# Keys and values of a linear attention in seven block products, sums formed in filled PSUM banks, and reciprocals in a compact form

## The chip, the cores and the metric

The kernel runs on one core of a Trainium2 chip. The metric is the device time of one execution in microseconds (us); three runs of the kernel before took 2869.28 to 2871.71 us, with a median of 2870.33.

## The reference

Two attention blocks over the same sequence (2048 tokens, width 1024, 32 heads of 32) are mixed by a gate for each token. All of it is in 32-bit floats.

```python
def _A_ref(x, wqkv, wo):                       # linear attention
    q, k, v = qkv[0], qkv[1], qkv[2]           # from x @ wqkv
    phi = lambda t: jnp.where(t > 0, t + 1, jnp.exp(t)) + 1e-6
    pq, pk = phi(q), phi(k)
    kv = jnp.einsum("bhsd,bhse->bhde", pk, v)
    z = jnp.einsum("bhsd->bhd", pk)
    num = jnp.einsum("bhqd,bhde->bhqe", pq, kv)
    den = jnp.einsum("bhqd,bhd->bhq", pq, z)[..., None] + 1e-6
    return (num / den, heads joined) @ wo
def _B_ref(x, wqkv, wo):                       # softmax attention
    scores = jnp.einsum("bhqd,bhkd->bhqk", q, k) * (Dh ** -0.5)
    p = _softmax(scores, axis=-1)
    return (jnp.einsum("bhqk,bhkd->bhqd", p, v), heads joined) @ wo
x = A_x
g = _sigmoid((x * gate_w).sum(-1, keepdims=True))
return g * _A_ref(x, A_wqkv, A_wo) + (1 - g) * _B_ref(x, B_wqkv, B_wo)
```

## The kernel before

Matmuls against weights are done in three passes: an operand is split into a high part (ScalarE rounds it, L252 or L547) and a low part (VectorE or GpSimd subtracts, L253 or L549), and high by high, high by low and low by high are summed in one bank (L146 to L148 in `three`). One product of a 128-token tile with 512 columns over a depth of 1024 is 8 x 3 = 24 matmuls of 128 x 128 by 128 x 512.

The stages in order:

- *First stage*, to about 400 us: X is loaded transposed and split. The first half of the softmax block's values is made (L446 to L448), and its queries and keys for pairs of 512-token blocks in seven products in place of eight (L407 to L409): the blocks of X are `x11` to `x22`, and four sums of them, `t1` to `t4`, are formed on VectorE and split as well (`v_next`, `v_sums`). The parts of X go to DRAM (`spill`), the sums don't.
- *Linear work*, a stream of chunks (`linear`): the second half of the values (`v`, alone on TensorE to about 525 us), four chunks `kv` of the linear attention (256 columns of keys beside 256 of values, L772 and after), two chunks `q`, two chunks `o` (the linear attention's output, its small matrices having been multiplied into the output weights by `mix`, L649).
- *Heads* (`heads_`, `maxima`), from 525 us on, beside the linear work: for each of 32 heads, 64 matmuls for the scores (L887) of which VectorE takes row maxima (L892); the maxima are turned, and go into two more rows of the queries; 64 matmuls for the transposed scores less the maxima (L1038), of which ScalarE takes exponentials (L1042) into one of seven SBUF tiles `pr` (one for each 128 keys); P·V in groups of five or six of these tiles (L1136, into the fixed bank 4). The row sums: GpSimd adds the first 1536 of 2048 columns of each tile to an accumulator (L1085, L1089), VectorE the rest in bank 7 (L1096, L1098). `finish` multiplies them by ones (L940), so that each of four rows of sums stands on 32 partitions, takes reciprocals of all 128 x 512 in four pieces (L947), multiplies the head's output by them (L950) and stores it (L952).
- *Output* (`output`), from about 2650 us: the softmax block's output projection, the gate and the store.

The order of every engine's instructions is written out ahead by a planner in the kernel. It keeps a clock for each engine (`T`, advanced by `use` with a cost written at each place) and at each step advances that stream (linear, maxima, heads, output) which is furthest behind its aim; `rates` holds how many matmuls of linear work go to one 512-column exponential. VectorE's work that nobody waits for at once is put off (`defer`) and run in a place that `fill` finds, or when its result is wanted (`need`). Six banks (`RING`) are handed out by `take` and given back by `give`. All DMAs are issued by SP, in the order of the program. `load_xp` loads the two split parts of a tile of X two tiles ahead; `load_w` and `split_w` load and split weights; `keys` multiplies phi(k) by v (L584) and adds the result to `kvb` (L593); `load_mix` loads output weights for `mix`, which is not started until 8 us of the planner's time later.

## Time and profile before

| | |
|---|---|
| median of three runs | 2870.33 us |
| the profiled execution | 2873.77 us |
| its span, first to last instruction | 2872.0 us |
| mean granted TensorE clock | 0.996 |
| moved by DMA | 400.57 MB |

In the page, PE is TensorE's matmuls and PEld its weight loads; DVE is VectorE, ACT ScalarE, POOL GpSimd, SP the engine that issues the DMAs. A group of instructions is a line of the kernel, an engine, an operation, and the tiles written and read (`mx<-bank`), with their shapes; behind the count stand the busy time in all, the mean time of one in ns, and how long the engine was idle just before them, with what ended that. An fp32 matmul such as those of L1136 has two records. Matmuls overlap in the records, so that the time of one is longer than the step from one to the next. The chain of waits is followed back from the last instruction, each time to what released it.

### The profile page before, as it was taken

Reading aid. Unit: us, or ns where it says so; the run is one execution under the profiler, and the core shown is the slowest. Engines: PE = TensorE matmul, PEld = TensorE weight load, DVE = VectorE, ACT = ScalarE, POOL = GpSimd, SP = SyncE. Lnnn points to the kernel's source line nnn. Section 1 sums busy time; section 2 is a strip of 40 time slices with the busy share of each in tenths; the row PEclk is TensorE's granted clock in tenths of the full one; section 3 lists DMA queues with packets and bytes.
Section 4 is the critical chain, followed back from the end, with each engine's and each line's share of the span. In section 5 each row is a group of like instructions: output and inputs, shape, how many; then the busy total and the mean of one; then the engine's idle time right before and its main releaser. Section 6 shows DMA issues by size and latency. Waiting matters only on the chain.

```text
span 2872.0 us, 44436 instructions
## 1 busy us (share of the span) xinstructions
PE 2846.1 (99%) x15744; PEld 2036.8 (71%) x15744; DVE 2239.1 (78%) x3775; ACT 1617.8 (56%) x3007; POOL 1854.1 (65%) x646
## 2 busy tenths in 40 slices
PE   9999999999999999999999999899999999999999
PEld 8888888666666666666666666566766666666687
DVE  7667656788888888888888888778888888886643
ACT  5334321666666667666666666566666656656421
POOL 1212220778898889888988887578778877885000
PEclk9999999999999999999999999999999999999999
DMA  5956764332333233333332235554465344524663
GB/s 179 284 174 212 247 201 152 121 93 92 108 89 92 89 101 110 90 92 92 120 93 90 76 120 168 173 185 145 135 195 167 114 137 133 144 88 143 213 219 105
DMA packets 302498, 400.57 MB, mean 139 GB/s; under 512 B 92682, under 2 KB 185354, under 8 KB 299146
## 3 DMA queue, kind: packets, MB, share of 16 engines
q1 hardware_dynamic: 302276, 397.73, 44.8%
q8 instruction: 124, 2.03, 0.3%
q14 instruction: 98, 0.80, 0.1%
HBM read 287.57 MB, written 108.79 MB: 138 GB/s over the span
## 4 chain that ended last, share of the span: by engine, by line
PE 96%; DMA 2%; DVE 1%; ACT 0%; issue 0%; SPq 0%; ACTq 0%; DVEq 0%
PE bank L1038 16%; PE bank L887 16%; PE bank L1136 15%; PE bank L146 11%; PE bank L148 11%; PE bank L147 11%; PE bank L407 4%; PE bank L409 4%; PE bank L408 4%; PE bank L446 1%; PE bank L940 1%; PE bank L447 1%; PE bank L448 1%; DMA big<-xs 1%; PE bank L693 0%; PE bank L584 0%
## 5 line engine op out<-in xcount | busy, mean ns | idle before, releaser
L1089 POOL TENSOR_TENSOR big<-big,big 128x1536 f32<-128x1536 f32 (+1 forms) x434 | 1556.4, 3586 | 188.9 <-ACT big L1042 166.7
L892 DVE TENSOR_REDUCE mx<-bank 128x1 f32<-128x512 f32 x2048 | 1311.4, 681 | 319.6 <-PE bank L887 315.1
L1042 ACT ACTIVATE big<-bank 128x512 f32<-128x512 f32 x2048 | 1180.6, 601 | 524.8 <-PE bank L1038 455.6
L1038 PE MATMUL bank<-big,big 128*128 128x512 f32 x2048 | 810.7, 397 | 2.7 <-ACT big L1042 2.6
L887 PE MATMUL bank<-big,big 128*128 128x512 f32 x2048 | 803.6, 392 | 3.2 <-ACT mid L342 2.9
L146 PE MATMUL bank<-big,big 128*128 128x512 f32 x1408 | 552.7, 393 | 5.7 <-DMA big<-xs 3.4
L148 PE MATMUL bank<-big,big 128*128 128x512 f32 x1408 | 550.9, 391 | 1.0 <-DMA big<-oA 0.6
L147 PE MATMUL bank<-big,big 128*128 128x512 f32 x1408 | 550.6, 391 | 0.0
L1038 PEld LDWEIGHTS bank<-big,big 128*128 128x128 f32 x2048 | 384.6, 188 | 159.7 <-issue 62.0
L1136 PE MATMUL bank<-big,mid 128*32 128x512 f32 x4096 | 461.1, 595 | 0.0
L887 PEld LDWEIGHTS bank<-big,big 128*128 128x128 f32 x2048 | 385.4, 188 | 87.4 <-ACT big L1042 3.7
L1136 PEld LDWEIGHTS bank<-big,mid 128*32 128x32 f32 x4096 | 127.9, 110 | 266.2 <-issue 266.2
L146 PEld LDWEIGHTS bank<-big,big 128*128 128x128 f32 x1408 | 264.6, 188 | 71.0 <-ACT big L1042 4.3
L148 PEld LDWEIGHTS bank<-big,big 128*128 128x128 f32 x1408 | 264.8, 188 | 57.6 <-DMA big<-oA 1.0
L147 PEld LDWEIGHTS bank<-big,big 128*128 128x128 f32 x1408 | 264.5, 188 | 55.3
L1098 DVE TENSOR_TENSOR bank<-bank,big 128x512 f32<-128x512 f32 (+1 forms) x434 | 280.6, 647 | 7.8 <-ACT big L1042 6.1
L1085 POOL TENSOR_TENSOR big<-big,big 128x1536 f32<-128x1536 f32 (+1 forms) x31 | 111.6, 3601 | 253.0 <-ACT big L1042 135.5
L253 DVE TENSOR_TENSOR big<-mid,big 128x512 fp32r<-128x512 f32 x216 | 153.0, 732 | 80.5 <-ACT big L252 80.5
L386 POOL TENSOR_TENSOR mid<-mid,mid 128x512 f32<-128x512 f32 x16 | 20.6, 1291 | 276.7 <-DVE big L253 250.6
L252 ACT CAST big<-mid 128x512 fp32r<-128x512 f32 x216 | 130.2, 624 | 95.8 <-POOL mid L387 54.0
L407 PE MATMUL bank<-big,big 128*128 128x512 f32 x448 | 174.3, 389 | 0.0
L408 PE MATMUL bank<-big,big 128*128 128x512 f32 x448 | 174.3, 389 | 0.0
(103 smaller groups left out, 1981.9 us busy)
## 6 DMA issues: line engine op xcount, KB each, us to landing
big<-xs SPq DMA_DIRECT2D x208, 512.0 KB
qk<-mid SPq DMA_DIRECT2D x128, 256.0 KB
big<-oA SPq DMA_DIRECT2D x64, 512.0 KB
big<-qk SPq DMA_DIRECT2D x96, 256.0 KB
big<-qk SPq DMA_DIRECT2D x384, 64.0 KB
mid<-in_b_wqkv SPq DMA_DIRECT2D x88, 256.0 KB
xs<-big SPq DMA_DIRECT2D x64, 256.0 KB
oA<-mid SPq DMA_DIRECT2D x64, 256.0 KB
```

The lines of the kernel that those rows point to most:

```text
L146: yield nc.tensor.matmul(ps, sh, mh_, start=(kt == 0), stop=False)
L147: yield nc.tensor.matmul(ps, sh, ml_, start=False, stop=False)
L148: yield nc.tensor.matmul(ps, sl, mh_, start=False, stop=(kt == NK - 1))
L407: nc.tensor.matmul(ps, sh, mh_, start=(i == 0), stop=False)
L408: nc.tensor.matmul(ps, sh, ml_, start=False, stop=False)
L887: nc.tensor.matmul(bank[b], q[:, t * P:(t + 1) * P], k[:, j * C:(j + 1) * C], start=True, stop=True)
L892: nc.vector.tensor_reduce(m[:, t, j:j + 1], bank[b], AX.X, ALU.max)
L1038: nc.tensor.matmul(bank[b], k[:, t * P:(t + 1) * P], q[:, j * C:(j + 1) * C], start=True, stop=True)
L1042: nc.scalar.activation(pr_t[i][:, j * C:(j + 1) * C], bank[b], AF.Exp, scale=SCALE)
L1089: nc.gpsimd.tensor_add(lacc[:, :qp], lacc[:, :qp], pr(t)[:, :qp])
L1098: nc.vector.tensor_add(lacc[:, qp:] if t == NT - 1 else l_b[:, :n], l_b[:, :n], src)
L1136: nc.tensor.matmul(av_b[j * DH:(j + 1) * DH, :], v[:, t, :], pr(t)[:, j * C:(j + 1) * C], start=(t == 0), stop=(t == NT - 1))
```

## The change

- *Keys and values.* Two chunks `kv` in place of four, each two old chunks wide (set `s`). Tokens are taken in eight pairs of tiles (`tokens`), 512 tokens apart, so that the parts and sums of X from the first stage serve again; the sums are now also stored (`spill_t`, 64 more stores in the first stage). A set has seven weight operands, `b11`, `b21`, `b22` and the sums `t1` to `t4`, which `w_sums` forms on GpSimd and stores (the first set's during the chunk `v`, the second's during the first set). A product is half as deep: 4 x 3 = 12 matmuls. `ORDER` takes them phase by phase, eight pairs in each.
- *Sums in banks.* The products must be added to each other. Where a sum starts from an earlier one, ScalarE copies that from SBUF into a free bank and the product's matmuls accumulate onto it (`get`, `start` false). A sum that is wanted again is copied out by ScalarE (`copy_u`) and stored to DRAM for a later phase (`load_u` brings it back); two products in every pair and set are added by VectorE (`add_u`). Only a bank that a whole 512-column matmul has written last may be filled so (`whole`). What was done at once behind each `kv` tile (phi, sums of keys) is a stream of its own, `kvout`.
- *Weights* of these products have their low parts taken by VectorE in place of GpSimd.
- *Reciprocals.* For all heads but the last, ScalarE copies the row sums to SBUF, four DMAs take one partition of each row to a tile of 128 x 16, VectorE takes reciprocals of that, a DMA stores them and one brings them back spread over 32 partitions for each row, and GpSimd multiplies the head's output by them (`back`, `scale`).
- *Planner.* Linear work may run ahead by 40 in place of 9; 1.5 matmuls of keys and values go to an exponential; the mixing is started 25 us after its loads in place of 8; VectorE's put-off work goes ahead of a maximum only if it ends 1 us before that can start, in place of 1 us after; between streams that all wait, the lag of ScalarE or VectorE counts too.

The core of the diff:

```diff
-AHEAD = {"head": 0, "max": 6, "lin": 9, "out": 0}
+RATE_KV = 1.5
+AHEAD = {"head": 0, "max": 6, "lin": 40, "kvout": 0, "out": 0}
...
-LATE = 1.0
+LATE = -1.0
...
+    NSET, NPAIR = 2, NT // 2
...
+    def take(seed=False, part=False, kept=False):
+
+        idle = [b for b in RING if not held[b] and (whole[b] or not seed)]
...
         return b
...
+    def spill_t(np_, i):
+
+        def one(name, p):
+            nc.sync.dma_start(xt_d[name][p][np_][:, :, i, :].rearrange("t p c -> p t c"),
+                              f32(xop(name, p, i)).rearrange("p (t c) -> p t c", c=P))
+
+        return [lambda a=(name, p): one(*a) for name in ("t1", "t2", "t3", "t4") for p in range(2)]
...
+    PHASES = ((("b11", "x"), ("b21", "x")), (("t2", "t2"),), (("t3", "t1"), ("t4", "x")), (("t1", "t3"), ("b22", "t4")))
+    WOPS = [op for ph in PHASES for op, _ in ph]
+    JOBS = [(ph, pair) for ph in range(len(PHASES)) for pair in range(NPAIR)]
...
+    def load_op(n, i):
...
+        s, m = divmod(n, len(WOPS))
+        if s == NSET:
+            return load_w("q", 0, m * HK + i, LEAD_W + 1)
+        op = WOPS[m]
+        if op[0] == "b":
+            raw = load_cols(a_wqkv, kv_cols(2 * s + int(op[2]) - 1), (int(op[1]) - 1) * HK + i, LEAD_W + 1)
+        else:
+            raw = raw_tile(LEAD_W + 1)
+            nc.sync.dma_start(raw, wt_d[s][op][i])
+        return raw, T["pe"] + 4.0
...
+    def w_sums(s, i, tiles):
+
+
+        r11, r12, r21, r22 = tiles
+
...
+        def loads():
+            for half, c, r in ((0, 0, r11), (0, 1, r12), (1, 1, r22), (1, 0, r21)):
+                load(r, half, c)
+
+        def add(fn, out, a, b):
+            use("pool", 1.29)
+            fn(out, a, b)
+
+        def store(name, r):
+            nc.sync.dma_start(wt_d[s][name][i], r)
+
+        sub, plus = nc.gpsimd.tensor_sub, nc.gpsimd.tensor_add
+        return ([loads],
+                [lambda: add(sub, r11, r11, r12), lambda: add(plus, r12, r22, r12),
+                 lambda: add(sub, r22, r22, r11), lambda: add(sub, r21, r21, r22)],
+                [lambda n=n, r=r: store(n, r) for n, r in (("t1", r11), ("t3", r12), ("t2", r22), ("t4", r21))])
+
+    w_steps = deque()
...
+    def kv_out(c, b, items=(), at=0.0):
+
+        n = n_kv[0]
+        n_kv[0] += 1
...
+        yield lambda: ended(items)
+        need(items)
+        yield from keys_alone(n - 2)
+        nc.scalar.copy(va, ps[:, HC:])
+        use("act", 0.28, T["pe"] + LATENCY["pe"], ended(items), at)
+        end = phi(ps, e, HC)
...
+    def load_u(what, pair, i):
+        nc.sync.dma_start(u_free(i), u_d[what][pair])
+        u_what[i] = what, pair
+        u_at[i] = T["pe"] + 4.5
+
+    def copy_u(i, b, what, pair):
+        u = u_free(i)
+        u_at[i] = use("act", 0.5, T["pe"] + LATENCY["pe"])
+        nc.scalar.copy(u, bank[b])
+        u_what[i] = what, pair
+        if what in (S1, U2, P7):
+            nc.sync.dma_start(u_d[what][pair], u)
+        return u_at[i]
+
+    def add_u(i, b):
+        item = defer(lambda _: nc.vector.tensor_add(bank[b], bank[b], u_tiles[i]),
+                     max(T["pe"] + LATENCY["pe"], u_at[i]), 0.66, 0)
+        u_left[i].append(item)
+        return item
...
+    ORDER = []
+    for m in range(NPAIR + 1):
+        ORDER += [(0, pr, q) for pr, q in ((0, m), (1, m - 1)) if 0 <= q < NPAIR]
+    ORDER += [(1, 0, q) for q in range(NPAIR)]
+    ORDER += [(2, pr, q) for q in range(NPAIR) for pr in range(2)]
+    for m in range(NPAIR + 1):
+        ORDER += [(3, pr, q) for pr, q in ((0, m), (1, m - 1)) if 0 <= q < NPAIR]
...
+        SEED = {(0, 1): (S1, lambda q: q % 4), (1, 0): (S1, lambda q: q % 4), (2, 1): (U2, lambda q: q % 2 * 2),
+                (3, 0): (U2, lambda q: q % 2 * 2), (3, 1): (W5, lambda q: q % 2 * 2)}
...
+        def get(pi):
+            s, ph, m, pair = XS[pi]
+            seeded = (ph, m) in SEED
+            b = take(seed=seeded)
+            end = free[b]
+            if seeded:
+                what, tile_of = SEED[ph, m]
+                i = tile_of(pair)
+                assert u_what[i] == (what, pair)
+                end = use("act", 0.6, free[b], u_at[i])
+                nc.scalar.copy(bank[b], u_tiles[i])
+            got[pi] = b, seeded, end
...
+            if pi not in got:
+                yield lambda: ready(pi)
+                get(pi)
+            b, seeded, at = got.pop(pi)
...
+                (sh, sl), (wh, wl) = [half_x(pi, p)[:, k] for p in range(2)], [wpart(slot, p) for p in range(2)]
+                for j, (x_, w) in enumerate(((sh, wh), (sh, wl), (sl, wh))):
+                    nc.tensor.matmul(bank[b], x_, w, start=(k == 0 and j == 0 and not seeded),
+                                     stop=(k == HK - 1 and j == 2), skip_group_check=seeded)
+                    lin_pe(1.0)
...
+            load_x(pi + 4)
+            c = 2 * s + (ph == 3)
+            if (ph, m) == (0, 0):
+                give(b, copy_u(pair % 4, b, S1, pair))
+            elif ph == 1:
+                give(b, copy_u(pair % 4, b, U2, pair))
+            elif (ph, m) == (2, 0):
+                give(b, copy_u(pair % 2 * 2 + 1, b, P7, pair))
+            elif (ph, m) == (2, 1):
+                kv_outs.append(kv_out(c, b, [add_u(pair % 2 * 2 + 1, b)]))
+            elif (ph, m) == (3, 0):
+                copy_u(pair % 2 * 2, b, W5, pair)
+                kv_outs.append(kv_out(c, b, [add_u(pair % 2 * 2 + 1, b)], u_at[pair % 2 * 2]))
+            else:
+                kv_outs.append(kv_out(c, b))
...
-        def store(_):
-            nc.vector.tensor_mul(avs, avs, pl)
-            for j in range(NJ):
-                nc.sync.dma_start(oB_d[j * TPC:(j + 1) * TPC, rows, g, :].rearrange("t p c -> p t c"),
-                                  avs[j * DH:(j + 1) * DH, :].rearrange("p (t c) -> p t c", c=P))
...
+        if h < H - 1:
+            part = l_part[h % 2]
+            end = use("act", 0.5, end)
+            nc.scalar.copy(l_sb, pl)
+            give(b, end)
+            for j in range(NJ):
+                nc.sync.dma_start(part[j * DH:(j + 1) * DH, :],
+                                  l_sb[j * DH:j * DH + 1, :].rearrange("o (c e) -> o c e", e=C // DH))
+
+            def back(end):
+                nc.vector.reciprocal(part, part)
+                nc.sync.dma_start(r_d[h % 2].rearrange("j (c e) -> (j c) e", e=C // DH), part)
+                nc.sync.dma_start(l_sb, r_d[h % 2].unsqueeze(1).to_broadcast([NJ, DH, C]))
+                scale_at[0] = end + 6.0
+
+            def scale():
+                need(f_left)
+                use("pool", 1.29)
+                nc.gpsimd.tensor_mul(avs, avs, l_sb)
+                for j in range(NJ):
+                    nc.sync.dma_start(oB_d[j * TPC:(j + 1) * TPC, rows, g, :].rearrange("t p c -> p t c"),
+                                      avs[j * DH:(j + 1) * DH, :].rearrange("p (t c) -> p t c", c=P))
+
+            f_left[:] = [defer(back, end + 4.0, 0.2, 2)]
+            task = (lambda: both(ended(f_left), scale_at[0]), scale)
+            f_task.append(task)
+            tasks.append(task)
+            return
...
-    rates["kv"] = rates["o"] = (cost["kv"] + cost["o"] - RESERVE) / (steps - cost["q"] / RATE_Q)
+    rates["kv"] = RATE_KV
+    rates["o"] = (cost["o"] - RESERVE) / (steps - cost["q"] / RATE_Q - cost["kv"] / RATE_KV)
```

TensorE, keys and values beside heads, before: `bank_249` collects one tile's product (L146 to L148) between scores (L887) and transposed scores (L1038), then row sums (L940), keys by values (L584) and P·V (L1136).

```order
2965 L147 MATMUL bank_249<-big_225,big_213 128x512
2966 L1038 MATMUL bank_245<-big_208,big_211 128x512 [waits Activation_49]
2967 L148 MATMUL bank_249<-big_225,big_213 128x512
...
2970 L887 MATMUL bank_246<-big_209,big_210 128x512 [waits DVE_49]
2971 L146 MATMUL bank_249<-big_226,big_213 128x512
2972 L940 MATMUL bank_245<-big_3756,ones 32x512 [waits Activation_49,Pool_49]
...
2974 L584 MATMUL bank_244<-mid_234,mid_236 32x32 [waits DVE_49]
...
2976 L1136 MATMUL bank_247<-big_3755,mid_241 32x512 x4
```

The same place now: L990 is the new products' line, L1386 the transposed scores, L1201 the scores, L685 keys by values.

```order
2327 L1386 MATMUL bank_302<-big_260,big_261 128x512 [waits DVE_49]
2328 L990 MATMUL bank_301<-big_279,big_264 128x512
2329 L1201 MATMUL bank_296<-big_263,big_262 128x512 [waits Activation_49]
2330 L1386 MATMUL bank_298<-big_260,big_261 128x512 [waits DVE_49]
2331 L990 MATMUL bank_301<-big_279,big_264 128x512
2332 L990 MATMUL bank_297<-big_276,big_264 128x512 [waits DMAHW4_49,Activation_49]
2333 L1201 MATMUL bank_299<-big_263,big_262 128x512 [waits DVE_49]
...
2335 L990 MATMUL bank_297<-big_276,big_264 128x512
...
2337 L685 MATMUL bank_298<-mid_284,mid_288 32x32 [waits Activation_49,Pool_49]
```

A product's first matmul (row 2332) now waits for ScalarE, and keys by values stand among the other matmuls in place of just ahead of P·V.

VectorE, the end of a head, before: the four reciprocals of the row sums and the scaling stand between the maxima (L892) of the next heads.

```order
2516 L892 TENSOR_REDUCE mx_200<-bank_245 128x1
2517 L698 TENSOR_TENSOR mid_238<-bank_249,mid_237 128x512
2518 L947 RECIPROCAL bank_243<-bank_243 128x128 x4
2519 L950 TENSOR_TENSOR mid_240<-mid_240,bank_243 128x512
2520 L892 TENSOR_REDUCE mx_200<-bank_243 128x1
```

And now, with L1211 the maxima, L1294 the small reciprocal and L1448 VectorE's share of the sums of probabilities:

```order
3019 L1211 TENSOR_REDUCE mx_250<-bank_301 128x1
3020 L1211 TENSOR_REDUCE mx_250<-bank_302 128x1
3021 L1294 RECIPROCAL l_part_256<-l_part_256 128x16
3022 L1448 TENSOR_TENSOR bank_303<-bank_303,big_3940 128x512
...
3026 L1448 TENSOR_TENSOR bank_303<-bank_303,big_3937 128x512
3027 L1211 TENSOR_REDUCE mx_250<-bank_299 128x1
```

One small instruction takes the place of five, and the shares of several tiles follow it in a row; before they stood singly among the maxima.

More of the change, by code (lines that the diff above doesn't have):

```diff
@@ L225, in take @@
         held[b] = True
+        whole[b] = whole[b] if kept else not part
         return b
@@ L503 @@
                     pass
-        for _ in side:
-            pass
+        while spills:
+            spill()
     while here:
@@ L670 @@
     z_end = [0.0, 0.0]
+    z_left = [[] for _ in range(2 * NSET)]
     def keysum(c):
-        yield lambda: both(bank_at(), z_end[c % 2])
-        b = take()
+        z_wait.remove(c)
+        need(z_left[c])
+        b = take(part=True)
         pz = bank[b]
@@ L688, in queries @@
         turned.add(n)
-        b = take()
+        b = take(part=True)
         pt = bank[b]
@@ L707, in linear @@
+    coming, loaded = deque(), deque()
     def linear():
         extra = iter(())
-        coming_w = deque()
+        coming_w = loaded
+        for i in range(HK):
+            steps = w_sums(0, i, [mid[m] for m in (3, 4, 5, 6)])
+            w_steps.extend([lambda fs=fs: [f() for f in fs] for fs in steps])
         for n, (i, t) in enumerate(units):
             kind, c = chunks[i]
-            pos = n % NT
+            if kind == "kv":
+                if n == KV0:
+                    lin_kind[0] = kind
+                    streams["kvout"] = kv_outputs()
+                    starts["kvout"] = next(streams["kvout"])
+                    yield from kv_all()
+                    yield lambda: None if sum(k_count) < 2 * NSET * NT or z_wait else 0.0
+                    del streams["kvout"], starts["kvout"]
+                continue
+            pos = t if kind != "v" else n
@@ L890, in maxima @@
                 fill(end + LATE)
+                while True:
+                    fit = [it for it in later if it.rank <= 1 and due(it) and it.at <= T["dve"]]
+                    if not fit:
+                        break
+                    run(min(fit, key=lambda it: (it.rank, it.at)))
                 give(b, use("dve", 0.605, end))
@@ L899, in turn @@
         def turn():
-            b = take()
+            b = take(part=True)
             pm = bank[b]
@@ L1067 @@
     pr_end = [0.0] * NPR
+    own_last = [None]
     def attend(h, lacc):
@@ L1360 @@
             wait = max(at - T["pe"], 0.0)
-            key = (wait > 0.02, wait if wait > 0.02 else -lag)
+            busy = max(T["dve" if name == "max" else "act"] - T["pe"], 0.0) if name in ("max", "head") else 0.0
+            key = (wait > 0.02, wait + TIE * busy if wait > 0.02 else -lag, wait)
             if best is None or key < best[0]:
```

269 lines of the change are left out of this document (211 added, 58 removed).

## The prediction

> **What bounds the kernel now.** I read the page's head first, then the stages by windows, then the groups of one stage, and last the timeline, to see whether a busy TensorE is a full one.
>
> ```profile
> span 2872.0 us, 44436 instructions
> PE 2846.1 (99%) x15744; PEld 2036.8 (71%) x15744; DVE 2239.1 (78%) x3775; ACT 1617.8 (56%) x3007; POOL 1854.1 (65%) x646
> ...
> PE 96%; DMA 2%; DVE 1%; ACT 0%; issue 0%; SPq 0%; ACTq 0%; DVEq 0%
> ```
>
> TensorE is idle for 25.9 of 2872.0 us and carries 96% of the chain. By stages (start:end, length, then busy us of PE, PEld, DVE, ACT, POOL, the granted clock, DMA share, GB/s), keys and values beside heads, queries beside heads, output projection beside heads:
>
> ```profile
> 525.00:1710.00 1185.00, 1185.00 (x7418) 803.85 (x7417) 1012.72 (x1724) 775.52 (x1499) 1036.74 (x368) 1.00 0.32 97
> 1710.00:2150.00 440.00, 426.07 (x2309) 297.39 (x2306) 362.82 (x632) 267.66 (x505) 321.40 (x89) 0.98 0.51 161
> 2150.00:2600.00 450.00, 448.98 (x2470) 304.52 (x2470) 380.24 (x618) 283.33 (x495) 365.12 (x104) 1.00 0.44 131
> ```
>
> In the first, which the change rewrites, TensorE has no gap at all; the next are GpSimd with 1036.74/1185 = 87% and VectorE with 85%. A recorded matmul lasts 0.39 us but overlaps the next, so I take the price from start to start: 36 steps lie between the first and the last row here,
>
> ```profile
> 400.01 0.39 PE L146 MATMUL bank<-big,big 128*128 128x512 f32 x1
> ...
> 408.17 0.39 PE L146 MATMUL bank<-big,big 128*128 128x512 f32 x1
> ```
>
> that is 8.16/36 = 0.2267 us each. A group of P·V (L1136), and the step into it and out of it:
>
> ```profile
> 2495.03 0.39 PE L887 MATMUL bank<-big,big 128*128 128x512 f32 x1
> 2495.35 5.36 PE L1136 MATMUL bank<-big,mid 128*32 128x512 f32 x48
> 2500.64 0.50 PE L1038 MATMUL bank<-big,big 128*128 128x512 f32 x1
> 2500.98 0.40 PE L148 MATMUL bank<-big,big 128*128 128x512 f32 x1
> ```
>
> 5.29 us for six key tiles of 8 records, 0.882 each; the steps of 0.32 and 0.34 beside it are 0.21 us more than two plain ones: what one excursion into another kind of matmul costs. TensorE's groups in 525 to 1710 us:
>
> ```profile
> L1038 PE MATMUL bank<-big,big 128*128 128x512 f32 x1174 | 465.4, 397 | 0.0
> L887 PE MATMUL bank<-big,big 128*128 128x512 f32 x1175 | 460.0, 391 | 0.0
> L1136 PE MATMUL bank<-big,mid 128*32 128x512 f32 x2384 | 266.5, 593 | 0.0
> L146 PE MATMUL bank<-big,big 128*128 128x512 f32 x503 | 197.2, 392 | 0.0
> L148 PE MATMUL bank<-big,big 128*128 128x512 f32 x503 | 197.0, 392 | 0.0
> L147 PE MATMUL bank<-big,big 128*128 128x512 f32 x503 | 196.9, 391 | 0.0
> L940 PE MATMUL bank<-big,ones 128*32 128x512 f32 x144 | 19.2, 605 | 0.0
> L584 PE MATMUL bank<-mid,mid 128*32 128x32 f32 x1008 | 19.1, 199 | 0.0
> ```
>
> 1174 + 1175 + 3 x 503 = 3858 matmuls x 0.2267 = 874.6; 2384/8 x 0.882 = 262.8; 19.2 and 19.1: together 1175.7 of 1185 us. So no hidden slack lies under "busy": a matmul taken away here is 0.2267 us off the end, if the others follow.
>
> **The change, part by part.** *Products.* Keys and values were 4 chunks x 16 token tiles x 24 = 1536 matmuls; now 2 sets x 7 products x 8 pairs x 12 = 1344. The 192 that go give 192 x 0.2267 = **-43.5 us**, all on the path. The Trainium skill (TensorE: Matmul & The Clock Gate, Back-to-back issue gap) gives about 131 ns for each in a sustained stream of weight load and 512-column matmul; by that figure the 192 would be worth an estimated 25 us and the end would come 18 us later than I say. The 36 steps above say 226.7 ns, and they decide.
>
> *Order on TensorE.* Counting the program order, the runs of one kind of matmul between others go from 157 to 175: 18 excursions x 0.21 = **+3.7 us**.
>
> *Filled banks.* Added: 80 copies from SBUF into a bank ahead of a product, 64 copies out of a bank, 32 additions in a bank. Nearest rows for them, and those of the reciprocals:
>
> ```profile
> L1144 ACT COPY mid<-bank 128x512 f32<-128x512 f32 x32 | 18.8, 588 | 151.7 <-PE bank L1136 136.0 <-DMA big<-qk 15.7
> L471 DVE TENSOR_TENSOR bank<-bank,big 128x512 f32<-128x512 f32 x16 | 11.0, 687 | 2.8 <-PE bank L409 2.8
> L947 DVE RECIPROCAL bank<-bank 128x128 f32<-128x128 f32 x128 | 123.3, 963 | 3.5 <-PE bank L940 0.4
> L950 DVE TENSOR_TENSOR mid<-mid,bank 128x512 f32<-128x512 f32 x31 | 21.3, 686 | 1.0
> L809 DVE RECIPROCAL dn<-dn 128x16 f32<-128x16 f32 x32 | 7.6, 238 | 0.4 <-ACT dn L805 0.4
> L549 POOL TENSOR_TENSOR big<-big,big 128x512 fp32r<-128x512 f32 x27 | 34.7, 1295 | 3.6 <-ACT big L547 3.6
> L892 DVE TENSOR_REDUCE mx<-bank 128x1 f32<-128x512 f32 x2048 | 1311.4, 681 | 319.6 <-PE bank L887 315.1
> L1042 ACT ACTIVATE big<-bank 128x512 f32<-128x512 f32 x2048 | 1180.6, 601 | 524.8 <-PE bank L1038 455.6
> ```
>
> ScalarE gets 144 x 0.588 = 84.7 us, and 31 more copies of row sums, 18.2; it waited 455.6 us for TensorE before its exponentials, which covers that in sum. What is queued behind such a copy is the next exponential, and behind that the banks of the scores. A copy that is late holds TensorE: at most 0.588 us x 80 = 47 us if every one shows, nothing if all are made during the product before, as the planner asks for; below nothing it can't be, as no wait goes with it. The nearest row is that of the stage, 0.0 idle over 64 tiles that had their own ScalarE work: I take **+2**.
>
> *VectorE.* Out: 124 reciprocals x 0.963 and 31 products x 0.686 = 140.7. In: 31 small reciprocals x 0.238, 32 additions x 0.687, 56 more subtractions for weights x 0.687 = 68. So some 72 us less, hidden beside TensorE: VectorE waited 315.1 us for it already. This buys room, not time.
>
> *GpSimd.* 32 subtractions fewer, 32 weight sums and 31 scalings more, each 1.295: +40 us, of which 16 sums fall before the heads, where it is idle. Room is least in the last stage. There the order holds 58 linear matmuls a head in place of 86: TensorE (128 + 58) x 0.2267 + 17 x 0.882 = 57.2 us a head, against
>
> ```profile
> 2414.39 21.38 POOL L1089 TENSOR_TENSOR big<-big,big 128x1536 f32<-128x1536 f32 x6 [2.06 <-ACT big L1042]
> ```
>
> 15 x 21.38/6 = 53.5, and 1.3 for the scaling: 54.8 us, 96%. Room of 2.4 us a head, and seven probability tiles to smooth it.
>
> *The small reciprocals' trip.* Row sums go ScalarE, SBUF to SBUF (four loads), VectorE, to DRAM, back to SBUF, GpSimd. Three waits are added. VectorE's small reciprocal waits for four loads, with its own share of the probability sums (L1098) and the maxima queued behind it; it stands ahead of a P·V group, when VectorE has nothing from TensorE. SP's load waits for the store just before it, with the loads of X for the products behind, which are four products ahead. GpSimd's scaling waits for the load, with the sums of probabilities behind, which free the tiles that the exponentials write. In the order it stands after seven or eight sums of the next head, about three (10.7 us) after the row sums. Transfers in this trace, issue to landing, in the busiest stage, and four issues of SP:
>
> ```profile
> 1845.39 8.03 DMA big<-xs
> 1907.34 5.22 DMA big<-xs
> 1912.62 6.57 DMA oA<-mid
> ```
>
> ```profile
> 2457.39 2.14 SPq L952 DMA_DIRECT2D oB<-mid  x4
> ```
>
> Between the 2.14 and 6.57 us for each of three, the trip takes 7 to 20.5 us with the copy and reciprocal. I take the low end, since those long ones are 512 KB or more in a queue at 0.5 to 0.95 busy: **+4 us** in all.
>
> *DMAs.* 570 more on SP, most of them in stages with a share of 0.32, hence nothing there. The first 500 us (share 0.66 to 0.72) get 64 stores of 256 KB and the weight sums. If that cover goes it looks like this stretch at 0.95, where TensorE lost 0.4 us in 10:
>
> ```profile
> 1920.00:1930.00 10.00, 9.57 (x59) 3.97 (x60) 5.54 (x10) 4.88 (x11) 5.24 (x2) 0.83 0.95 280
> ```
>
> 0 to 21 us; I take **+2**, as the raw tiles are loaded well ahead.
>
> *The mixing loads.* The planner now allows 25 us in place of 8 for them. What that wait cost before:
>
> ```profile
> PE bank L649 <- DMA big<-in_a_wo: 7.5, 1, 7.5
> ```
>
> ```profile
> 1825.00:1830.00 5.00, 0.52 (x2) 0.19 (x3) 0.00 (x0) 0.00 (x0) 0.00 (x0) 0.55 0.50 162
> 1830.00:1835.00 5.00, 5.00 (x44) 1.09 (x46) 0.99 (x2) 1.61 (x4) 0.00 (x0) 0.50 0.05 15
> ```
>
> 7.5 us of idling and 5 us at a clock of 0.50, so 10 us. It can stay (0) or go (-10); landing took 12.2 us on the chain, under 25: **-9**.
>
> *Sum.* The profiled execution took 2873.8 us (span 2872.0), 3.4 above the median of the three runs. 2873.8 - 43.5 + 3.7 + 2 + 4 + 2 - 9 = 2833.0, less 3.4: **2830 us** (about 1.4% less).
>
> **The rivals.**
> *GpSimd stalls on the trip* (slower). With 6.57 us for each transfer the trip is 20.5 us and GpSimd stands 9.8 us a head at the scaling; less the room of 2.4, 7.4 us x 11 heads of the last stage = 81: about 2907 us. It costs the whole gain from (40/11) + 2.4 = 6 us of standing a head, transfers of some 5.3 us. For it: 96%. Against: only 2.14 us to issue four, small transfers, and 0.44 of DMA share there.
> *The filled banks show* (no change). If nearly all 80 copies lie open, 2830 - 2 + 47 = 2875 us. For it: ScalarE is in order, behind exponentials. Against: products of eight pairs in one phase are independent, and scores and maxima stand between their matmuls.
> *GpSimd already is the bound* (slower). If busy matmuls hid waits for GpSimd and VectorE, taking matmuls away would give nothing, and GpSimd's own net of about +19 us beside the heads (31 x 1.295 + 16 x 1.295 - 32 x 1.295) would come on top: 2889 us. The Trainium skill (Perfetto Trace Analysis, Identifying the Most-Contended Engine) holds matmul busy time for a poor measure of headroom and asks for the weight loads' share, here 71%, so it would look at GpSimd first. Against: 1175.7 of 1185 us are accounted for from start to start.
>
> **How the numbers follow.** Forecast 0.83, stalls on the trip 0.07, filled banks 0.06, GpSimd the bound 0.04. About 0.2%, 5.7 us, is what a measurement here can tell from no change. Faster 0.83, within 0.06 (filled banks), slower 0.11. Low end: no new wait and the full 10 us, 2821, and half of the other 18 us of idle time gone as the order shifts, 2812. High end: the forecast with 28 us more of waits (21 of them the DMA's bound, or more than half of the copies open), 2858.
>
> **What would show it.** Right: TensorE still about 99% busy, 1344 matmuls of the new line at 0.2267 us, no wait at the mixing, waits for filled banks under 5 us, VectorE about 72 us less busy and GpSimd 40 more. Wrong: TensorE's waits name ScalarE's copy, or exponentials wait for GpSimd's sums while GpSimd waits for the load of reciprocals; or a first stage longer than 525 us.

## The result, and the profile after

The kernel after took 2975.36 us (median of four runs, 2972.17 to 2979.18), 1.0363 times the time of before (95% interval 1.0350 to 1.0376): 105 us slower, where 40 us faster was forecast. The head of its page and its chain:

```profile
span 2970.4 us, 45541 instructions
PE 2858.2 (96%) x15552; PEld 2017.0 (68%) x15552; DVE 2314.5 (78%) x3739; ACT 1690.5 (57%) x3206; POOL 1899.5 (64%) x677
...
PE 86%; DMA 6%; DVE 4%; ACT 1%; issue 1%; SPq 1%; POOL 0%; DVEq 0%; ACTq 0%
```

The 192 matmuls are gone (15552 records for 15744), but TensorE is idle for 2970.4 - 2858.2 = 112 us in place of 26, and VectorE, which was to be 72 us less busy, is 75 more. (Busy time counts records that overlap once. The lengths of VectorE's instructions, added up one by one, come to 2468 us in both kernels: the 72 us less did not come, and fewer records overlap.) The transposed scores of the first head begin at 521 us in place of 504. The stages of keys and values, queries, and output projection beside heads (columns as in the prediction):

```profile
525.00:1555.00 1030.00, 980.57 (x6055) 658.30 (x6053) 877.16 (x1375) 694.06 (x1397) 817.05 (x302) 0.98 0.48 142
1555.00:2030.00 475.00, 456.22 (x2442) 317.35 (x2442) 379.36 (x662) 284.32 (x546) 345.82 (x98) 0.98 0.51 160
2200.00:2600.00 400.00, 393.28 (x2188) 258.87 (x2187) 357.11 (x557) 261.62 (x468) 357.48 (x107) 0.99 0.38 112
```

The stage that the change rewrites had no gap before; now it has 49 us of them, at a clock of 0.98. Whom TensorE waited for (us in total, times, longest):

```profile
PE bank L1386 <- DVE mx L1211: 19.9, 11, 3.4
PE bank L1386 <- DMA big<-m_both: 14.7, 3, 8.0
PE bank L158 <- DMA big<-xs: 10.2, 4, 5.1
PE bank L990 <- ACT bank L944: 10.1, 5, 7.2
...
PE bank L1201 <- DMA big<-qk: 6.4, 1, 6.4
```

First stand the maxima. VectorE's groups of one new kind of work say why. Here is the same operation before, then after (L549 became L636), and then the first of the two groups of after with its shortest, median and longest time in ns:

```profile
L549 DVE TENSOR_TENSOR big<-mid,big 128x512 fp32r<-128x512 f32 x8 | 5.5, 692 | 5.2 <-ACT big L547 5.1
```

```profile
L636 DVE TENSOR_TENSOR big<-big,big 128x512 fp32r<-128x512 f32 x37 | 66.6, 1805 | 9.7 <-ACT big L634 9.5
L636 DVE TENSOR_TENSOR big<-mid,big 128x512 fp32r<-128x512 f32 x27 | 31.8, 1178 | 15.6 <-ACT big L634 7.9 <-DMA big<-xs 7.7
```

```profile
L636 DVE TENSOR_TENSOR big<-big,big x37: 674/1066/3952, 636.0 to 1554.2; 128x512 fp32r<-128x512 f32 x37
```

The subtraction that takes a weight's low part needs 0.674 us at its shortest and 3.952 at its longest. The eight of before stood about 500 us, where GpSimd did nothing. Of the 64 of after, 24 overlap no instruction of GpSimd and take 0.67 to 0.69 us. The 25 that take over 1 us all overlap one, and end 0.55 us after it. One of the long ones in the timeline of after:

```profile
637.34 4.54 DVE L636 TENSOR_TENSOR big<-big,big 128x512 fp32r<-128x512 f32 x2
637.43 3.90 POOL L1439 TENSOR_TENSOR big<-big,big 128x1536 f32<-128x1536 f32 x1 [1.16 <-ACT big L1390]
...
639.18 0.39 PE L1201 MATMUL bank<-big,big 128*128 128x512 f32 x1
641.81 3.07 DVE L1211 TENSOR_REDUCE mx<-bank 128x1 f32<-128x512 f32 x5
642.54 0.50 PE L1386 MATMUL bank<-big,big 128*128 128x512 f32 x1 [2.97 <-DVE mx L1211]
```

The line of 4.54 us holds two subtractions: the first takes 0.67 us, the second 3.94. It ends at 641.88, 0.55 us after GpSimd's addition does (637.43 + 3.90); alone the two would take 1.4 us. Five maxima are queued behind them, and TensorE stands 2.97 us for a bank. The Trainium skill (SBUF — State Buffer, Who interferes with whom) has a rule for this: a VectorE instruction with two SBUF inputs and a GpSimd instruction that reads SBUF exclude each other, and the later one stands until the first is through. These rows agree with it. VectorE's maxima and its additions in banks have one SBUF input or none, and keep their length beside GpSimd: 1775 of the maxima overlap it and take 0.686 us on average, as do the 273 that don't.

### The profile page after: what moved, and what is told of

Read it like the earlier page. It is cut to its first block, busy times and chain, and to the rows that moved or that the text cites. A ratio compares the mean times of both kernels' runs of the same rounds, so it can differ in the third digit from the quotient of the medians.

```text
span 2970.4 us, 45541 instructions
## 1 busy us (share of the span) xinstructions
PE 2858.2 (96%) x15552; PEld 2017.0 (68%) x15552; DVE 2314.5 (78%) x3739; ACT 1690.5 (57%) x3206; POOL 1899.5 (64%) x677
## 4 chain that ended last, share of the span: by engine, by line
PE 86%; DMA 6%; DVE 4%; ACT 1%; issue 1%; SPq 1%; POOL 0%; DVEq 0%; ACTq 0%
PE bank L1386 15%; PE bank L1201 14%; PE bank L1487 14%; PE bank L990 9%; PE bank L158 6%; PE bank L160 6%; PE bank L159 6%; PE bank L435 3%; PE bank L433 3%; PE bank L434 3%; DVE mx L1211 1%; DVE big L636 1%; PE bank L1269 1%; PE bank L471 1%; PE bank L472 1%
## 5 line engine op out<-in xcount | busy, mean ns | idle before, releaser
L1211 DVE TENSOR_REDUCE mx<-bank 128x1 f32<-128x512 f32 x2048 | 1335.0, 686 | 305.9 <-PE bank L1201 297.1
L1390 ACT ACTIVATE big<-bank 128x512 f32<-128x512 f32 x2048 | 1157.1, 602 | 459.4 <-PE bank L1386 407.1
L1386 PE MATMUL bank<-big,big 128*128 128x512 f32 x2048 | 816.3, 402 | 55.1 <-DVE mx L1211 19.9
L1201 PE MATMUL bank<-big,big 128*128 128x512 f32 x2048 | 811.2, 397 | 20.8 <-ACT big L1390 7.2
L1386 PEld LDWEIGHTS bank<-big,big 128*128 128x128 f32 x2048 | 386.1, 189 | 226.8 <-issue 63.8
L1487 PE MATMUL bank<-big,mid 128*32 128x512 f32 x4096 | 467.5, 602 | 0.0
L990 PE MATMUL bank<-big,big 128*128 128x512 f32 x1344 | 457.0, 400 | 10.3 <-ACT bank L944 10.1
L1201 PEld LDWEIGHTS bank<-big,big 128*128 128x128 f32 x2048 | 388.9, 190 | 113.4 <-DVE mx L1211 14.2
L158 PE MATMUL bank<-big,big 128*128 128x512 f32 x896 | 355.9, 397 | 12.7 <-DMA big<-xs 10.2
L159 PE MATMUL bank<-big,big 128*128 128x512 f32 x896 | 354.5, 396 | 1.6 <-DMA big<-wa 1.5
L160 PE MATMUL bank<-big,big 128*128 128x512 f32 x896 | 353.9, 395 | 1.4 <-DVE big L267 1.4
L990 PEld LDWEIGHTS bank<-big,big 128*128 128x128 f32 x1344 | 257.3, 192 | 68.0 <-ACT bank L944 13.4
L1448 DVE TENSOR_TENSOR bank<-bank,big 128x512 f32<-128x512 f32 (+1 forms) x434 | 283.5, 653 | 24.4 <-ACT big L1390 1.6
L158 PEld LDWEIGHTS bank<-big,big 128*128 128x128 f32 x896 | 170.6, 190 | 55.6 <-issue 12.7
L159 PEld LDWEIGHTS bank<-big,big 128*128 128x128 f32 x896 | 170.8, 191 | 38.7 <-DMA big<-wa 3.7
L160 PEld LDWEIGHTS bank<-big,big 128*128 128x128 f32 x896 | 170.7, 191 | 38.5 <-DVE big L267 1.8
```

The lines of the kernel that those rows point to most:

```text
L158: yield nc.tensor.matmul(ps, sh, mh_, start=(kt == 0), stop=False)
L159: yield nc.tensor.matmul(ps, sh, ml_, start=False, stop=False)
L160: yield nc.tensor.matmul(ps, sl, mh_, start=False, stop=(kt == NK - 1))
L990: nc.tensor.matmul(bank[b], x_, w, start=(k == 0 and j == 0 and not seeded), stop=(k == HK - 1 and j == 2), skip_group_check=seeded)
L1201: nc.tensor.matmul(bank[b], q[:, t * P:(t + 1) * P], k[:, j * C:(j + 1) * C], start=True, stop=True)
L1211: nc.vector.tensor_reduce(m[:, t, j:j + 1], bank[b], AX.X, ALU.max)
```

## The experiments

Ratios are to the kernel before in the same job (2871.3 to 2873.1 us), with the 95% interval in brackets.

### The weights' low parts, and the reciprocals

Each of the two is tested in the kernel after and in the kernel before. **a_pool** is the kernel after with one word changed:

```diff
-                    split_w(None, None, slot, *loaded.popleft(), nc.vector)
+                    split_w(None, None, slot, *loaded.popleft(), nc.gpsimd)
```

> The changed kernel with one part undone: the low parts of the keys' and values' weights are again taken by GpSimd. Theory A (in the changed kernel's trace the 64 subtractions of L636 on VectorE take 0.674 to 3.95 us, 98.4 us in all against 64 x 0.69 = 44 if alone; the long ones lie over a GpSimd sum of 3.5 us and end with it, and TensorE then waits for banks that VectorE's maxima hold): the keys and values' stage loses 60 to 90 us of its 100 lost, 2885 to 2915 us, unless GpSimd, which gets some 72 us more, becomes the bound. Theory B (the trip of the small reciprocals holds VectorE, GpSimd and the rows of maxima): at most 15 us of change, 2960 or more. Theory C (more DMAs, filled banks, the planner's new numbers): 2960 or more.

2903.53 us, 1.0117 [1.0102, 1.0132]: 72 us less than after, and still 32 more than before. TensorE's first wait in the list above has become:

```profile
PE bank L1386 <- DVE mx L1211: 9.4, 1, 9.4
```

The planner counts each subtraction on the engine that takes it, so this word also changes the order that it writes. **b_dve** is the kernel before, with all its low parts on VectorE:

```diff
-                    split_w(*follow, k, *coming_w.popleft(), nc.vector if kind == "v" else nc.gpsimd)
+                    split_w(*follow, k, *coming_w.popleft(), nc.vector)
```

> The kernel before with the low parts of all linear weights on VectorE (40 subtractions moved from GpSimd). Theory A: each stands 0.9 us on average behind a GpSimd sum as in the changed kernel, some up to 3.9 us, with VectorE 85% busy: 20 to 50 us slower, 2890 to 2920 us, with L549 on VectorE at a mean over 1.2 us. Theories B and C: 2865 to 2880.

2920.53 us, 1.0173 [1.0158, 1.0188]: +49 us for 40 subtractions more. In its groups the same operation:

```profile
L549 DVE TENSOR_TENSOR big<-big,big 128x512 fp32r<-128x512 f32 x27 | 36.6, 1363 | 6.8 <-ACT big L547 6.8
L549 DVE TENSOR_TENSOR big<-mid,big 128x512 fp32r<-128x512 f32 x21 | 25.2, 1201 | 6.3 <-ACT big L547 6.2
```

48 of them take 61.8 us; at 0.69 they would take 33. The 34 that overlap no instruction of GpSimd take at most 0.69 us, the other 14 together 38.8. So the cost is there without the seven products. That it passes through the maxima shows in the gaps of over 0.15 us before TensorE's weight loads, from 500 to 2700 us: those that end with a maximum come to 49 us in place of 8, those that end with an exponential to 23 in place of 18. No run keeps the 40 subtractions on VectorE but away from GpSimd, so the split between their lengthening and their mere number is read from the traces. **a_oldrec** puts the old reciprocals back into the kernel after, **b_rec** the compact ones into the kernel before:

```diff
-        if h < H - 1:
-            part = l_part[h % 2]
...
+        def store(_):
+            nc.vector.tensor_mul(avs, avs, pl)
```

> The changed kernel with one part undone: reciprocals of all 128 x 512 on VectorE and its scaling as before, no trip. Theory A: VectorE, already late in the keys' stage, gets 4.5 us more a head: 2975 to 3010 us. Theory B: 30 us or more come back, 2945 or less. Theory C: within 15 of 2975.

> The kernel before with the compact reciprocals alone (row sums by ScalarE and DMAs, small reciprocal on VectorE, scaling on GpSimd). Theory A: 2860 to 2880 us, since VectorE wasn't the bound. Theory B: 2895 to 2930 us. Theory C: 2860 to 2880.

a_oldrec: 3021.80 us, 1.0524 [1.0506, 1.0541], 46 us more than after and above every range given. b_rec: 2911.37 us, 1.0138 [1.0123, 1.0153], 40 us more than before, as the trip's theory had it. So the trip is dear in the old order, and yet the compact form helps in the new one. What it costs in the old order, in the waits of VectorE and of TensorE in b_rec:

```profile
DVE l_part L978 <- DMA l_part<-l_sb: 138.9, 30, 16.6
```

```profile
PE bank L149 <- DMA big<-xs: 18.9, 6, 5.8
PE bank L1070 <- DVE mx L895: 11.8, 3, 10.9
```

VectorE stands 4.6 us in each of 30 heads for the four small loads. **a_pool_oldrec** has the old reciprocals and the low parts on GpSimd, with the diffs above. As a_oldrec does, it leaves out one thing that the old reciprocals need: it counts the bank of the row sums as written whole, so that a product may start from it. What counts is its time:

> The kernel after with the weights' low parts on GpSimd, and the old reciprocals (all 128 x 512 on VectorE, no trip) in place of the compact ones. The kernel with the low parts on GpSimd alone took 2903.5 us, 73 above my forecast; what makes up the 73 is open. Theory D (the trip's waits, in SP's queue above all: the head's stores wait for GpSimd, the loads of X and of the turned maxima stand behind): the trip goes, as its 40 us did not exist in the kernel before, and the time falls to 2840-2870. Theory E (the seven products' own order: filled banks that are late, the first stage's DMAs): the trip is not the cause, VectorE gets its 72 us back, and the time stays within 15 us of 2903 or rises, 2890-2950.

2941.06 us, 1.0246 [1.0230, 1.0261]: D falls, as far as it names the trip as what makes a_pool slow.

### SP's order and the plan

**a_pool_gq** is a_pool with the head's four stores issued by GpSimd, **a_aq** has the four small loads issued by ScalarE as well:

```diff
                 nc.gpsimd.tensor_mul(avs, avs, l_sb)
                 for j in range(NJ):
-                    nc.sync.dma_start(oB_d[j * TPC:(j + 1) * TPC, rows, g, :]...
+                    nc.gpsimd.dma_start(oB_d[j * TPC:(j + 1) * TPC, rows, g, :]...
...
-                nc.sync.dma_start(part[j * DH:(j + 1) * DH, :], ...
+                nc.scalar.dma_start(part[j * DH:(j + 1) * DH, :], ...
```

> The kernel after with the weights' low parts on GpSimd, and the four stores of a head's output, which wait for GpSimd's scaling, issued by GpSimd itself in place of SP. SP waited 182 us for that scaling in 30 places (10.6 us at most). Theory D: SP's queue was what was late; the time falls by 10-30 us to 2875-2893, and the waits of TensorE for X, for the turned maxima and for loads of sums shrink. Theory E: within 5 us of 2903.5. If GpSimd's own issue of a DMA costs it 1 us or more, 4 x 31 of them are 120 us of GpSimd, and the time rises to 2910-2950.

> The kernel with low parts on GpSimd and stores issued by GpSimd (2890.5 us), and now the four small loads of row sums issued by ScalarE, right behind its own copy, in place of SP. In that kernel's trace VectorE stood 11.5 us at a small reciprocal, as SP reached the four loads late, with maxima queued behind, and TensorE stood 9.4 us for them. Theory D (SP's order makes the trip dear): 2870-2884. Theory E: 2888-2894. Four more issues a head on ScalarE could cost up to 0.3 us each of an engine with 40% idle: no more than +5.

2890.52 us, 1.0065 [1.0050, 1.0080], so 13 us for the first; 2890.43, 1.0062 [1.0045, 1.0079], nothing for the second. Where the second was aimed at, in the timeline of a_pool_gq:

```profile
2056.76 8.33 SPq L1172 DMA_DIRECT2D big<-qk  x3
...
2060.00 0.40 PE L160 MATMUL bank<-big,big 128*128 128x512 f32 x1
2065.18 2.47 SPq L1290 DMA_DIRECT2D l_part<-l_sb  x4
2068.91 0.25 DVE L1294 RECIPROCAL l_part<-l_part 128x16 f32<-128x16 f32 x1 [11.50 <-DMA l_part<-l_sb]
...
2069.76 0.80 PE L1386 MATMUL bank<-big,big 128*128 128x512 f32 x1 [9.37 <-DVE mx L1211]
```

SP is held at three loads (8.33 us), so that the small loads go out late, VectorE stands 11.50 us at a reciprocal of 0.25, and TensorE 9.37 us for the maxima behind it. It is the longest stall of its kind in the run. In a_aq, whose small loads don't pass through SP, TensorE's wait of 9.37 us is gone, and the time is the same. The four issues took ScalarE 0.60 us each (median), twice what was allowed for. **a_aq2** plans the small reciprocal later and starts the first weight sum one tile later, and **a_aq_num** gives a_aq the two numbers of before:

```diff
-            f_left[:] = [defer(back, end + 4.0, 0.2, 2)]
+            f_left[:] = [defer(back, end + 8.0, 0.2, 2)]
...
-            if kind == "v":
+            if kind == "v" and n > 0:
                 w_step()
```

```diff
-AHEAD = {"head": 0, "max": 6, "lin": 40, "kvout": 0, "out": 0}
+AHEAD = {"head": 0, "max": 6, "lin": 9, "kvout": 0, "out": 0}
...
-LATE = -1.0
+LATE = 1.0
```

> The same with two moves of the plan: the small reciprocal is planned 8 us after the row sums in place of 4, and the first weight sum's eight loads start one tile later, so that they do not stand ahead of the first loads of queries and keys (TensorE waited 5.6 us for those). Theory D: another 8-15 us down, 2858-2874. Theory E: within 4 us of the kernel without them.

> The kernel with stores issued by GpSimd and small loads by ScalarE, and the planner's two numbers of before (linear work ahead by 9 in place of 40, put-off work up to 1 us past a maximum in place of 1 us short of it). If the new numbers are part of what is lost: 5-20 us less than with them. If they help: 5-20 us more. My prediction gave them nothing: within 4 us.

2883.69 us, 1.0038 [1.0023, 1.0053] and 2923.00, 1.0176 [1.0161, 1.0191]: the two new numbers together are worth 33 us beside the compact reciprocals, and the prediction put them at nothing. **a_rate123** and **a_rate136** are a_aq2 with another `RATE_KV`:

> The best of the kernels so far (low parts and head stores on GpSimd, small loads on ScalarE, small reciprocal planned later: 2883.7 us) with 1.23 matmuls of keys and values to an exponential in place of 1.5, so that the output projection has as many. If the last stages lose because they hold too little linear work for the heads' other engines (theory H): 2865-2878. If the loss belongs to the heads' other engines wherever the work lies (theory G): 2880-2888.

> The same with 1.36, half way. Theory H: 2870-2880. Theory G: 2880-2888.

2887.07 us, 1.0046 [1.0032, 1.0060], and 2881.74, 1.0033 [1.0020, 1.0045]. Where the linear work lies among the heads makes no difference that these runs can tell; theory H falls. None of these is faster than the kernel before.

### The terms of the forecast, one by one

**b_spill** and **b_mix** are the kernel before with the 64 stores, and with the mixing 25 us after its loads:

> The kernel before with the 64 stores of the sums of X added in the first stage (they are read by nobody) and the stores of X issued in the order of the kernel after; nothing else. My prediction gave these stores 2 us, and the heads begin 17 us later in the kernel after. Theory F (first stage's DMA load): 2880-2890. Otherwise: 2869-2876, and the late start belongs to the weight sums and the loads for the new products.

> The kernel before with the mixing planned 25 us after its loads in place of 8; nothing else. My prediction gave that -9 us (7.5 us of waiting and some 2.5 of a lower clock): 2859-2864. If the mixing's place moves other waits in: 2866-2876.

2873.73 us, 1.0011 [1.0002, 1.0020]: the stores cost 2.4 us, the prediction's 2. 2870.86 us, 0.9999 [0.9989, 1.0009]: no gain from the mixing. Its trace has lost the wait of 7.5 us for `in_a_wo`, and has these in its place:

```profile
PE bank L1038 <- DMA big<-ml: 4.5, 1, 4.5
PE bank L1038 <- ACT mid L822: 3.8, 1, 3.8
PE bank L903 <- ACT mid L822: 3.2, 1, 3.2
```

**a_prod** is the seven products alone, as near as they can be had (a_pool_oldrec with the two numbers of before, and the row sums' bank taken with `part=True`, that is, not counted as whole):

> The seven products alone, as near as they can be had: the kernel after with the weights' low parts on GpSimd, the old reciprocals on VectorE, and the planner's two numbers of before (linear work ahead by 9, VectorE's put-off work up to 1 us past a maximum); the bank of the row sums is no longer counted as whole. What stays of the change: products, filled banks, loads and stores of sums, weight sums, mixing after 25 us. By my forecast's terms (-43.5 products, +3.7 order, +2 filled banks, +2 DMAs) 2830-2845 us. Theory E (filled banks and VectorE's additions do not fit beside VectorE's old work): 2880-2945; with the numbers of the change and the same old reciprocals it was 2941.

2891.96 us, 1.0067 [1.0052, 1.0082]: 57 above the 2834 that the forecast's terms add up to, and its head shows hardly an idle TensorE:

```profile
span 2889.6 us, 45249 instructions
...
PE 2853.7 (99%) x15552; PEld 1986.2 (69%) x15552; DVE 2265.1 (78%) x3807; ACT 1678.0 (58%) x3175; POOL 1924.5 (67%) x702
```

**b_thin** takes the forecast's largest term by itself, in the kernel before:

```diff
-                for m, _ in enumerate(three(ps, stat, (wpart(k, 0), wpart(k, 1)), k)):
+                thin = kind == "kv" and k == NK - 1
+                for m, _ in enumerate(range(3) if thin else three(ps, stat, ...)):
```

> The kernel before, with the last of the eight depth blocks of every product of keys and values left out: 64 x 3 = 192 matmuls fewer, nothing else changed and the plan the same with holes (loads and splits are still made). It tests the forecast's largest term by itself. If each matmul taken away is 0.2267 us off the end: 2870 - 43.5 = 2825-2830. If the other engines do not follow (theory G, another engine paces the heads as soon as TensorE has less): 2845-2870.

2855.62 us, 0.9943 [0.9928, 0.9958]: 16 us for 192 matmuls, not 43.5. The same 900 us beside heads, before, and in b_thin:

```profile
600.00:1500.00 900.00, 900.00 (x5627) 610.84 (x5626) 770.25 (x1312) 589.83 (x1141) 792.79 (x283) 1.00 0.32 97
```

```profile
600.00:1500.00 900.00, 898.14 (x5546) 585.92 (x5549) 777.24 (x1329) 595.17 (x1154) 802.31 (x286) 1.00 0.33 97
```

TensorE reads as busy in both, with 81 records fewer in the second, and 25 us less of weight loads: the busy time has not moved, the work has. Where the time hides, in the timeline of b_thin:

```profile
743.85 0.40 PE L888 MATMUL bank<-big,big 128*128 128x512 f32 x1
744.09 0.42 PE L1039 MATMUL bank<-big,big 128*128 128x512 f32 x1
744.35 0.50 PE L888 MATMUL bank<-big,big 128*128 128x512 f32 x1
744.70 0.51 PE L1039 MATMUL bank<-big,big 128*128 128x512 f32 x1
745.04 0.40 PE L146 MATMUL bank<-big,big 128*128 128x512 f32 x1
```

Steps of 0.35 and 0.34 us stand among steps of 0.24 and 0.26. No gap shows, as the records overlap and those of a late matmul are longer. Counted over all steps from one 128 x 128 by 128 x 512 matmul to the next, from 500 to 2700 us, against 0.2267 us, 146 are late by 0.1 to 1 us before, 292 in b_thin and 423 in a_prod; together 21, 42 and 68 us. Whom they wait for stands in the rows of the weight loads (us in total, times, longest), before, in b_thin, and in a_prod:

```profile
PEld bank L1038 <- ACT big L1042: 9.2, 27, 3.1
```

```profile
PEld bank L1039 <- ACT big L1043: 19.7, 73, 1.0
PEld bank L888 <- ACT big L1043: 13.9, 50, 0.7
PEld bank L888 <- DVE mx L893: 8.2, 35, 0.5
```

```profile
PEld bank L1367 <- ACT big L1371: 32.8, 109, 2.6
PEld bank L1367 <- DVE mx L1211: 25.5, 78, 1.0
PEld bank L1201 <- DVE mx L1211: 16.2, 52, 1.0
```

They are the exponentials and the maxima, which free the banks of the scores. All such gaps of over 0.15 us before weight loads, from 500 to 2700 us, come to 26 us before, 69 in b_thin and 107 in a_prod; a part of each gap is usual between loads.

**a_nofill**, **a_norecip** and **a_pool1024** each leave one load out of a_prod:

```diff
-                nc.scalar.copy(bank[b], u_tiles[i])
...
-        nc.scalar.copy(u, bank[b])
...
-        item = defer(lambda _: nc.vector.tensor_add(bank[b], bank[b], u_tiles[i]),
+        item = defer(lambda _: None,
...
```

```diff
-            nc.vector.reciprocal(pl[:, sl], pl[:, sl])
+            h < H - 1 or nc.vector.reciprocal(pl[:, sl], pl[:, sl])
```

```diff
-            nc.gpsimd.tensor_add(lacc[:, :qp], lacc[:, :qp], pr(t)[:, :qp])
+            n = qp - 512
+            nc.gpsimd.tensor_add(lacc[:, :n], lacc[:, :n], pr(t)[:, :n])
```

> The seven products alone (2892 us), with the work around the filled banks left out: no copies into banks, no copies out of banks for later sums, no additions of VectorE in banks, no loads and stores of these sums; the products stand by themselves, the plan is the same with holes. Theory E (that work stands ahead of the exponentials and maxima and holds TensorE): 2835-2860. If it is hidden, as I forecast: 2885-2892.

> The seven products alone (2892 us), with the reciprocals of all heads but the last left out (124 of 0.963 us on VectorE, 4% of its load; the head's output is multiplied by the row sums themselves), the order of all else the same. If VectorE paces the heads in the new order: 2840-2870. If GpSimd or the filled banks do: 2882-2892.

> The seven products alone (2892 us), with GpSimd's sums of probabilities over 1024 of its 1536 columns from the third tile on (a third of 512 columns in each of some 450 additions left out), the order of all else the same. If GpSimd paces the heads: 2840-2870. It also frees VectorE's two-input subtractions and additions in SBUF sooner, which are few here. If VectorE or the filled banks do: 2882-2892.

2880.78 us, 1.0033 [1.0023, 1.0044]; 2881.38, 1.0031 [1.0021, 1.0042]; 2891.43, 1.0061 [1.0044, 1.0078]. Filled banks and the work around them cost 11 us, the reciprocals 11, and GpSimd, relieved of 475 us, nothing. The gaps that end with exponentials and maxima stay, at 99, 107 and 106 us. The page of a_pool1024:

```profile
PE 2854.7 (99%) x15552; PEld 1986.9 (69%) x15552; DVE 2262.6 (78%) x3807; ACT 1678.7 (58%) x3175; POOL 1449.1 (50%) x702
```

## Why the prediction was wrong

Two steps failed. The measured time lies above every rival too, of which the highest was 2907 us.

- **VectorE: "some 72 us less, hidden beside TensorE. This buys room, not time."** This step cost most: with the low parts back on GpSimd 72 us return (a_pool), enough by itself to turn 40 us faster into 32 slower; 40 subtractions cost 49 us in the old order (b_dve). The 56 more subtractions were priced at 0.687 us, from the row of L471. GpSimd read SBUF beside 14 of the 16 of that row, but one of its inputs is a bank: the row was near in shape and neighbour, not in where its operands lie. The subtraction has both inputs in SBUF. Beside GpSimd, busy for 817 of the stage's 1030 us with additions of 3.6 us above all, the 64 subtractions of after take 98.4 us in place of 44, with maxima behind them. The trace of before had both cases:

```profile
L1098 DVE TENSOR_TENSOR bank<-bank,big 128x512 f32<-128x512 f32 x364 | 251.0, 689 | 5.7 <-ACT big L1042 4.5
L253 DVE TENSOR_TENSOR big<-mid,big x216: 679/685/1545, 4.5 to 2692.0; 128x512 fp32r<-128x512 f32 x108
```

  The first, with a bank among its inputs, stands beside GpSimd's additions and keeps its length. Of the second, with both inputs in SBUF, 196 overlap no GpSimd instruction and take 0.69 us on average; 20 do and take 1.19, up to 1.545.
- **Products: "192 x 0.2267 = -43.5 us, all on the path".** The step time is right, that all of it is on the path isn't. In the old order 192 matmuls are worth 16 us (b_thin). The prediction took 1175.7 of 1185 us "accounted for" as proof of no slack; it proves that TensorE had no idle time then, not that the others could follow if it went faster. As matmuls go, waits for exponentials and maxima take their place. The clause "if the others follow" stood in the text without a price. The third rival (another engine already at its limit) was nearest to what happened and had a chance of 0.04; it put GpSimd first, which a_pool1024 rules out for the seven products. What the prediction cites there from the Trainium skill (Perfetto Trace Analysis, Identifying the Most-Contended Engine), that matmul busy time is a poor measure of headroom, agrees with b_thin, where busy time stays at 99% with 192 matmuls fewer.
- **Filled banks, +2 (0 to 47).** 11 us with all that belongs to them (a_nofill): inside the bounds, and the low end was chosen for a stage with no idle time, a stage that was about to change.
- **The trip, +4.** Mis-sized, and by place: +40 in the old order (b_rec), where VectorE stands 138.9 us for small loads. In the new order the kernels make a table: old reciprocals 2892 us with the old numbers (a_prod) and 2941 with the new ones (a_pool_oldrec, whose row sums' bank is counted as whole as well); compact ones 2923 (a_aq_num) and 2890 (a_aq), both with SP relieved. Each form has numbers that suit it, and the better ones of the two forms are equal. The first rival, GpSimd standing 9.8 us a head for the load of the reciprocals, is not what happened: it stood 34.4 us in five places of after. So no gain of the compact form in itself shows, and the two numbers of the *planner*, priced at nothing, are worth 33 us with it.
- **DMAs, +2.** Right for the stores (b_spill, +2.4). What I left out is SP's order: 13 us come back when the head's stores leave it (a_pool_gq), some 7 more with two moves of the plan (a_aq2, though the intervals overlap). The heads' later start is not the stores': TensorE waits 11.4 us for two loads at 417 and 507 us of after, where one wait of 2.9 us stood before.
- **The mixing, -9.** The wait went and the time did not (b_mix): other waits of 4.5, 3.8 and 3.2 us show in its place.
- **GpSimd, order of TensorE.** No run tests the +3.7 us of the order. GpSimd's 40 us more are covered in a_prod, where even 475 us less change nothing.

Together: the forecast without the mixing's gain, the trip and the reciprocals is 2834 us for a_prod. If b_thin's price holds in the new order, which no run tests, matmuls that are not worth their length take 27 us of the 57 above it. Filled banks take 9 more than forecast, and two waits for loads at the start of the heads 6 more than the 2.9 us of before (5.3 and 3.8):

```profile
PE bank L1201 <- DMA big<-qk: 5.3, 1, 5.3
PE bank L158 <- DMA big<-xs: 4.7, 2, 3.8
```

About 15 us stay open, as does which of VectorE's maxima and ScalarE's exponentials, and the banks between them, sets the pace of the heads: less VectorE work helps by a tenth of what is left out (116 us less busy, 11 us gained), and no single load that was left out gives the whole. For the kernel after, the 72 us of the subtractions and the 13 of SP's order are measured; the rest of the 145 us between 2830 and 2975 is not split by a run.

## What to carry to other kernels

Before an instruction is moved to another engine, look what its neighbour in time does there: a subtraction with both inputs in SBUF cost VectorE up to six times its length beside GpSimd's additions, and the row to price it by must have its operands in the same memories and such a neighbour beside it. A TensorE that reads 99% busy tells what it does now, not what a matmul less is worth. Take some out, with the order unchanged, before an algorithm is built on that price. Where a long wait is removed in an order that is written out, expect the next one in its place, and price the whole, not the wait.

## What the runs showed of the hardware

- A subtraction of 128 x 512 with both inputs in SBUF took VectorE up to 3.952 us beside a 128 x 1536 addition of GpSimd, and 0.674 alone; each of the 25 of over 1 us ended 0.55 us after GpSimd's instruction. An addition with one input in a bank (L1098 of before) kept 0.689 us beside the same additions.
- A late matmul's record is longer (0.50 and 0.51 us in place of 0.40), so that waits of 0.1 us leave no gap in TensorE's row; they show in the rows of its weight loads.
- After a stall of 9.37 us TensorE's 128 x 512 matmuls took 0.63 us in place of 0.40 in a_pool_gq, and followed each other after 0.42 or 0.43 us, at a granted clock of 0.65 from 2069.7 to 2074 us, so that a stall costs more than its own length:

```profile
2070.78 0.63 PE L1386 MATMUL bank<-big,big 128*128 128x512 f32 x1
2071.21 0.63 PE L158 MATMUL bank<-big,big 128*128 128x512 f32 x1
2071.64 0.63 PE L159 MATMUL bank<-big,big 128*128 128x512 f32 x1
```
